# Attention and two expert layers on one core: the last two chunks' rows written in two transfers, and another order of placing expert 0's rows

## The chip, the core and the metric

The kernel runs on one core of a Trainium2 chip. A core has five engines with instruction streams of their own: TensorE (PE, matmuls), VectorE (DVE), ScalarE (ACT), GpSimd (POOL) and SyncE (SP, which here only issues transfers). The streams run in order and wait for each other by semaphores. Transfers between the chip's memory and the on-chip memory run on 16 DMA engines. The metric is the device time of one run in microseconds.

## The reference

Three layers follow each other. Attention with a decaying state (2 batches, 8 heads, 768 tokens, 64 numbers per head), then a mixture of 8 experts in which a token is computed only if a skip score is positive, then a second mixture of 8 experts with a limit of tokens per expert.

```python
for t in range(S):
    state = gamma * state + einsum('bhd,bhe->bhde', k[:, :, t], v[:, :, t])
    y[:, :, t] = scale * einsum('bhd,bhde->bhe', q[:, :, t], state)
# x = y as 1536 rows of 512
do_compute = (x @ w_skip) > 0                      # first mixture
e_idx = argmax(xc @ w_gate)                        # xc: the rows that are computed
h = maximum(xc[mask] @ w1[e], 0.0)                 # 512 x 1024
out[do_compute] = xc + gate_w * (h @ w2[e])        # 1024 x 512
# second mixture: the same shapes, own weights; at most `capacity` rows per expert
```

## The kernel before

Attention runs in 6 chunks of 128 tokens (`NCH = 6`), each with two batches `b`. For every chunk a generator, `sink` in `route_tokens`, follows attention by some steps: it computes the router's logits of the chunk's 256 tokens, picks an expert for each, turns the tokens into rows, and writes the rows with their gates to `table`, an array in the chip's memory. A row of `table` is 516 numbers wide (`RW`): 512 of the token (`DM`), two gates (`GCOL`) and the token's number (`IDCOL`). Later every expert collects its 128 rows from `table` with an indirect transfer (`gather`, issued by GpSimd).

The generator's steps are put between the steps of attention by `step_side`; one step ends at each `yield`. So the order of the instructions on each engine is the order in which the Python code runs.

For chunks 0 to 4, `sink` does this: `logits` (4 matmuls with the router's weights, copied to `lgs` by ACT, L395), a yield, `summed` and `pick` (the choice, on DVE; `ex` on ACT) and `weigh` (the gates: `se` and the reciprocal, L325), a yield, `rows_T` for both batches (4 transposes on TensorE each, L409, and a copy to `rc` by ACT, L413), `write_rows` on ACT's queue (L355), a yield, and then the ranks of the tokens within their experts. In chunk 4, the last of these, it ends with a gather of its own: `a0` gets the rows that expert 0 has from chunks 0 to 4 (L362, with the ids of L477).

The last chunk, 5, has its own code, `last_chunk`. Its rows of expert 0 don't go through `table`: `place` puts them in their slots by a matmul with a one-hot matrix `oh` (L499, `late[0]` for batch 0, `late[1]` for batch 1), and adds `a0` through the identity matrix, all in two accumulators `acc[0]` and `acc[1]` that hold two of the four column blocks each (`KT = 4`, L372). `split` (ACT L378, then DVE L379) turns each accumulator into a high and a low part, `xh` and `xl`, with which the first expert's first layer begins (L794). `warm` is a matmul whose result nobody reads. Chunk 5's rows are written to `table` by SP (L355), ahead of two weight loads (L213) in SP's stream. All later experts' gathers need them.

Rows that are named `rowc_107` and `rowc_108` below are the row buffers of chunk 4 and of chunk 5; `big` are weights as loaded, `hi` and `lo` their parts, `xt` a chunk's attention result, `p` its masked scores, `a_105` the buffer `a0`, and `sbd` the state.

Of the kernel before, what the change touches and what calls it, by code (L numbers as in the profile page):

```python
# [15 lines left out]
B, H, S, D = 2, 8, 768, 64  # L16
NT, DM, E, FF = B * S, H * D, 8, 1024
NCH = S // 128
NTILE = NT // 128
KT = DM // 128  # L20
FT = FF // 128
RW = 516
# [19 lines left out]
def kernel(  # L42
# [12 lines left out]
    nc = tc.nc  # L55
# [9 lines left out]
    at = ExitStack()  # L65
# [3 lines left out]
    table = dram.tile([NROW, RW], F32, name="table")  # L69
# [46 lines left out]
    a0 = const.tile([128, RW], F32, name="a0")  # L116
# [4 lines left out]
    ident = cs[:, C_ID:C_ID + 128]  # L121
# [226 lines left out]

    done = [1]

    def write_rows(eng, src, n):

        r0 = done[0]
        done[0] += 128 * n
        eng.dma_start(out=table[r0:done[0], :].rearrange("(n p) w -> p n w", p=128), in_=src)  # L355

    def gather(at, n=None, t=None):

# [9 lines left out]
    def place(acc, rows, where, first, last, ks=range(KT)):  # L368

        n = KT // len(acc)  # L370
        for k in ks:
            nc.tensor.matmul(  # L372
                out=acc[k // n][:, 128 * (k % n):128 * (k % n) + 128], lhsT=rows[:, 128 * k:128 * k + 128], rhs=where,
                start=first and k % n == 0, stop=last, skip_group_check=True,
            )
# [9 lines left out]
    def route_tokens(rows, rows_p):  # L385
# [26 lines left out]
        def rows_T(xt, rc, b, psum):  # L412
            nc.scalar.activation(out=rc[:, b, 0:DM], in_=turned_rows(xt, b, psum), func=ACTF.Copy)  # L413
# [28 lines left out]
        def sink(c, xt, psum):  # L442
            if c == NCH - 1:
                yield from last_chunk(xt, psum)
                return
            rc = rows[c % len(rows)]
            bs = list(range(B))
            if not c:
                yield
            lgs = logits(xt, bs, psum)  # L450
            nc.gpsimd.tensor_copy(out=rc[:, :, IDCOL:IDCOL + 1], in_=tok[:, :, c:c + 1])
            yield
            lg = summed(lgs, B, psum)
            m, weigh = pick(lg, B, 2, None, rc[:, :, GCOL:GCOL + 2])
            m3 = m.rearrange("p (a g) j -> p a (g j)", a=B)
            weigh()
            rhs = numbers(nc.gpsimd, m3, c, bs)
            yield
            rows_T(xt, rc, 0, psum)
            if c < NCH - 2:  # L460
                yield
            rows_T(xt, rc, 1, psum)
            write_rows(nc.scalar, rc, B)
            yield
            rk = psum("s", 4)
            ranked(rk, lc[:, 0, :], m.rearrange("p n j -> p (n j)"), cum.rearrange("p a j -> p (a j)"))
            sl = slot(rk, m3, B)
            where = [slots_of(sl, i) for i in bs]
            for i in bs:
                counted(m3[:, i, :])  # L470
            yield
            if c < NCH - 2:
                yield
            for i in bs:
                to_slots(where[i], rhs[:, i], 0, 16)
            if c == NCH - 2:
                nc.vector.tensor_copy(out=ids_0[:, 0:1], in_=tab[:, 0:1])  # L477
                gather(ids_0[:, 0:1], t=a0)

        def last_chunk(xt, psum):  # L480

            c = NCH - 1
            rc = rows[c % len(rows)]
            nc.gpsimd.tensor_copy(out=rc[:, :, IDCOL:IDCOL + 1], in_=tok[:, :, c:c + 1])
            m, m2, rhs, late = {}, {}, {}, {}
            ex = ex9[2 * B]

            def picked(b, lgs):
                got, _ = pick(summed(lgs, 1, psum), 1, 2, None, None, ex[:, 2 * b:2 * b + 2])
                m[b] = got.rearrange("p (a g) j -> p a (g j)", a=1)  # L490
                m2[b] = got.rearrange("p n j -> p (n j)")
                rhs[b] = numbers(nc.gpsimd, m[b], c, [b])

            def ranks(b):
                rk = psum("s", 4)
                ranked(rk, lc[:, 0, :], m2[b], cum[:, 0, :], [m2[0]] if b else [])
                sl = slot(rk, m[b], 1)
                oh = rows_p.tile([128, 128], F32, tag="oh", name="oh")
                nc.vector.scalar_tensor_tensor(  # L499
                    out=oh, in0=iota[:, 0:128], scalar=sl[:, 0:1], in1=m[b][:, 0, 0:1].to_broadcast([128, 128]),  # L500
                    op0=ALU.is_equal, op1=ALU.mult,
                )
                late[b] = (rc[:, b, :], oh)
                return sl

            lgs = logits(xt, [0], psum)
            yield
            picked(0, lgs)
            yield
            xr = turned_rows(xt, 0, psum)  # L510
            sl = [ranks(0)]
            lgs = logits(xt, [1], psum)
            nc.scalar.activation(out=rc[:, 0, 0:DM], in_=xr, func=ACTF.Copy)
            warm(psum("s", 4), 1)
            picked(1, lgs)
            rows_T(xt, rc, 1, psum)
            warm(psum("s", 4), 1)
            sl.append(ranks(1))
            acc = [psum("m"), psum("m")]
            place(acc, *late[0], True, False)  # L520
            hi = x_p.tile([128, KT, 128], F32R, tag="xh", name="xh")
            lo = x_p.tile([128, KT, 128], F32R, tag="xl", name="xl")
            gate(ex, B, 2, rc[:, :, GCOL:GCOL + 2])
            write_rows(nc.sync, rc, B)
            for g in range(2):
                ks = slice(2 * g, 2 * g + 2)
                place(acc, *late[1], False, False, range(KT)[ks])
                place(acc, a0, ident, False, True, range(KT)[ks])
                split(acc[g][:, 0:256].rearrange("p (k t) -> p k t", k=2), hi[:, ks], lo[:, ks])
            x0.append((hi, lo))  # L530

            def gather_all():
                where = [slots_of(sl[b], 0, sm, "whereb", 2) for b in range(B)]
                for b in range(B):
                    to_slots(where[b], rhs[b][:, 0], 0, 16)
                nc.vector.tensor_copy(out=ids, in_=tab)
                for e in (1, 0, 2, 3):
                    xs1[e] = gather(ids[:, e:e + 1], 1 + NT)
                for b in range(B):
                    counted(m2[b])  # L540

            x0.append(gather_all)
            yield
# [3 lines left out]
    def warm(acc, n):  # L547

        for _ in range(n):
            nc.tensor.matmul(out=acc, lhsT=zb[:, 0:128], rhs=zb[:, 0:512], start=True, stop=True)  # L550
# [194 lines left out]
    def psum(tag="t", bufs=3):  # L745
        return ps.tile([128, 512], F32, tag=tag, bufs=bufs, name=tag)
# [269 lines left out]
    acc = run(second)  # L1016
    then_route(0, acc)
    for e in range(1, E):
# [12 lines left out]
        if e > 1:  # L1031
# [12 lines left out]
            acc = last_step(second, FT // 2 - (3 if e == E - 1 else 1))  # L1044
# [11 lines left out]
    acc = run(second)  # L1056
# [31 lines left out]
    acc = run(second)  # L1088
# [67 lines left out]
    acc = run(second)  # L1156
# [207 lines left out]
```

## Time and profile before

| | |
|---|---|
| median of 3 runs | 385.44 us (385.2 to 385.46) |
| profiled execution | 384.92 us, of which the span of the profile is 383.1 us |
| TensorE busy | 368.7 us, 96% of the span, granted clock 0.995 on average |
| DVE, ACT, GpSimd busy | 244.7, 213.8, 121.1 us |
| moved by DMA | 95.99 MB, 251 GB/s on average |

An engine's busy time counts its own instructions; waiting and issuing are not busy. The profile's view of the chain that ended last covers only the very end of this program, so stretches, waits and timelines have to tell what bounds the rest. Idle time of an engine that nobody waits for costs nothing. A wait is put down to the last semaphore event that the profile can see; where the engine named had long been done, it was another, often a transfer.

### The profile page before, as it was taken

How to read it: one execution, taken by the hardware profiler on the slowest of the kernel's cores; microseconds unless marked ns; L12 is line 12 of the kernel's file. 1: busy time of each engine (PE TensorE's matmuls, PEld its weight loads, DVE VectorE, ACT ScalarE, POOL GpSimd, SP SyncE). 2: the span in 40 equal slices, each digit the busy share in tenths (PEclk: the TensorE clock that was granted, in tenths of full speed). 3: DMA queues.
4: the chain of work that ended last, by engine and by line, in shares of the span. 5: the costliest groups of instructions: out<-in, count | busy, mean ns of one | idle time of the engine just before them, and what ended most of it. 6: DMA issues, size and time to landing. Idle time of an engine off the chain costs nothing. (4 is left out here: it accounts for less than half of the span.)

```text
span 383.1 us, 6796 instructions
## 1 busy us (share of the span) xinstructions
PE 368.7 (96%) x2641; PEld 311.0 (81%) x2642; DVE 244.7 (64%) x402; ACT 213.8 (56%) x317; POOL 121.1 (32%) x185
## 2 busy tenths in 40 slices
PE   8999999799999999999999999999999999999992
PEld 4788887587777787886678998989899898998981
DVE  3657786479896999899626982747627466473200
ACT  1446554387986777795338763646546454562110
POOL 2677773285042060233251402205031140401102
PEclk9999999999999999999999999999999999999998
DMA  8999976689999999988746784947748386110001
GB/s 292 423 418 399 357 216 230 190 316 379 394 390 397 372 342 350 344 298 323 275 117 188 256 323 150 322 162 216 285 143 307 110 289 242 60 44 28 26 3 43
DMA packets 18128, 95.99 MB, mean 251 GB/s; under 512 B 2401, under 2 KB 2657, under 8 KB 8616
## 3 DMA queue, kind: packets, MB, share of 16 engines
q1 hardware_dynamic: 12196, 80.85, 57.2%
q0 software_dynamic: 3280, 9.76, 8.1%
q10 hardware_dynamic: 2612, 4.86, 3.5%
q8 instruction: 23, 0.38, 0.4%
q14 instruction: 17, 0.14, 0.1%
HBM read 87.03 MB, written 9.48 MB: 252 GB/s over the span
## 5 line engine op out<-in xcount | busy, mean ns | idle before, releaser
L255 DVE TENSOR_TENSOR lo<-big,hi 128x1024 fp32r<-128x1024 f32 (+1 forms) x130 | 151.3, 1185 | 54.1 <-ACT hi L252 53.6
L252 ACT ACTIVATE hi<-big 128x1024 fp32r<-128x1024 f32 (+1 forms) x130 | 128.6, 1015 | 6.9 <-DMA big<-in_w1a_dram 4.0
L788 PE MATMUL s<-xh,lo 128*128 128x256 f32 x224 | 63.4, 283 | 0.0
L787 PE MATMUL s<-xl,hi 128*128 128x256 f32 x224 | 63.4, 283 | 0.0
L786 PE MATMUL s<-xh,hi 128*128 128x256 f32 x224 | 63.4, 283 | 0.0
L924 POOL DMA_INDIRECT out_dram<-y,ixo x16 | 18.6, 1165 | 138.6 <-ACT y L919 136.6
L786 PE MATMUL o<-hi,hTh 128*128 128x512 f32 x112 | 44.2, 394 | 0.0
L788 PE MATMUL o<-hi,hTl 128*128 128x512 f32 x112 | 43.6, 390 | 0.0
L787 PE MATMUL o<-lo,hTh 128*128 128x512 f32 x112 | 43.6, 389 | 0.0
L786 PEld LDWEIGHTS s<-xh,hi 128*128 128x128 f32 x224 | 43.0, 192 | 0.3
L787 PEld LDWEIGHTS s<-xl,hi 128*128 128x128 f32 x224 | 43.0, 192 | 0.3
L788 PEld LDWEIGHTS s<-xh,lo 128*128 128x128 f32 x224 | 43.0, 192 | 0.0
L1124 ACT ACTIVATE hTh<-s 128x512 fp32r<-128x512 f32 x28 | 16.7, 598 | 39.0 <-PE s L788 39.0
L1125 DVE SCALAR_TENSOR_TENSOR hTl<-s,hTh 128x512 fp32r<-128x512 f32 x28 | 19.3, 690 | 28.4 <-ACT hTh L1124 28.4
L919 ACT ACTIVATE y<-o,rowc 128x512 f32<-128x512 f32 (+1 forms) x15 | 10.1, 675 | 45.6 <-issue 29.3
L794 PE MATMUL s<-hi,xh 128*128 128x512 f32 x80 | 32.6, 408 | 0.9 <-DVE xl L379 0.9
L794 PE MATMUL s<-lo,xh 128*128 128x512 f32 x80 | 31.3, 391 | 0.0
L794 PE MATMUL o<-hi,hTh 128*128 128x512 f32 x72 | 29.7, 412 | 0.0
L794 PE MATMUL o<-lo,hTh 128*128 128x512 f32 x72 | 28.2, 391 | 0.0
L794 PE MATMUL s<-hi,xl 128*128 128x512 f32 x80 | 25.0, 394 | 0.0
L788 PEld LDWEIGHTS o<-hi,hTl 128*128 128x128 f32 x112 | 21.0, 188 | 4.4
L787 PEld LDWEIGHTS o<-lo,hTh 128*128 128x128 f32 x112 | 21.1, 188 | 4.2
(162 smaller groups left out, 604.0 us busy)
## 6 DMA issues: line engine op xcount, KB each, us to landing
big<-in_w1a_dram SPq DMA_DIRECT2D x16, 1024.0 KB, 8.8
big<-in_w2a_dram SPq DMA_DIRECT2D x16, 1024.0 KB, 7.1
big<-in_w1b_dram SPq DMA_DIRECT2D x16, 1024.0 KB, 5.4
big<-in_w2b_dram SPq DMA_DIRECT2D x16, 1024.0 KB, 6.0
qk<-in_qkv_dram SPq DMA_DIRECT2D x5, 1024.0 KB, 9.8
big<-in_qkv_dram SPq DMA_DIRECT2D x5, 1024.0 KB, 11.7
table<-rowc ACTq DMA_DIRECT2D x5, 516.0 KB, 6.5
table<-row ACTq DMA_DIRECT2D x3, 516.0 KB, 5.5
```

The lines of the kernel that those rows point to most:

```text
L252: nc.scalar.activation(out=hi[:, k], in_=r3[:, k], func=ACTF.Copy)
L255: nc.vector.tensor_tensor(out=lo[:, k], in0=r3[:, k], in1=hi[:, k].bitcast(F32), op=ALU.subtract)
L786: nc.tensor.matmul(out=acc, lhsT=a[0], rhs=w[0], start=first, stop=False)
L787: nc.tensor.matmul(out=acc, lhsT=a[0], rhs=w[1], start=False, stop=False)
L788: nc.tensor.matmul(out=acc, lhsT=a[1], rhs=w[0], start=False, stop=last)
L794: nc.tensor.matmul(out=acc, lhsT=a, rhs=w, start=first and i == 0, stop=last and i == len(todo) - 1)
L919: nc.scalar.activation(out=y[:, 0:n], in_=acc[:, 0:n], func=ACTF.Copy, scale=xs[:, GCOL + 1:GCOL + 2])
L924: new = nc.gpsimd.indirect_dma_start(out=out[:, :], out_offset=bass.IndirectOffsetOnAxis(ap=ix, axis=0), in_=y, in_offset=None, bounds_che ...
L1124: nc.scalar.activation(out=hi[:, g:g + 2, :], in_=acc, func=ACTF.Relu)
L1125: nc.vector.scalar_tensor_tensor(out=lo[:, g:g + 2, :], in0=acc, scalar=0.0, in1=hi[:, g:g + 2, :].bitcast(F32), op0=ALU.max, op1=ALU.subtract
```

## The change

In chunk 4 the transposes and the copies of the rows come right behind the logits, in the step before the choice is made. The 512 columns of the tokens are issued as one transfer there, and the 4 columns of gates and number as a second transfer once the gates are made; both are on ACT's queue. In chunk 5 the rows are written in the same two parts on SP's queue. And in chunk 5 one `warm` goes, the rows of batch 0 are placed before the ranks of batch 1 are made, and `a0` is placed whole before the rows of batch 1 instead of block by block behind them.

```diff
+    def next_rows(n):
         r0 = done[0]
         done[0] += 128 * n
-        eng.dma_start(out=table[r0:done[0], :].rearrange("(n p) w -> p n w", p=128), in_=src)
+        return table[r0:done[0], :].rearrange("(n p) w -> p n w", p=128)
+
+    def write_rows(eng, src, n):
+        eng.dma_start(out=next_rows(n), in_=src)
...
             lgs = logits(xt, bs, psum)
             nc.gpsimd.tensor_copy(out=rc[:, :, IDCOL:IDCOL + 1], in_=tok[:, :, c:c + 1])
+            if c == NCH - 2:
+                for b in bs:
+                    rows_T(xt, rc, b, psum)
+                at = next_rows(B)
+                nc.scalar.dma_start(out=at[:, :, 0:DM], in_=rc[:, :, 0:DM])
             yield
...
-            rows_T(xt, rc, 0, psum)
             if c < NCH - 2:
+                rows_T(xt, rc, 0, psum)
                 yield
-            rows_T(xt, rc, 1, psum)
-            write_rows(nc.scalar, rc, B)
+                rows_T(xt, rc, 1, psum)
+                write_rows(nc.scalar, rc, B)
+            else:
+                nc.scalar.dma_start(out=at[:, :, DM:RW], in_=rc[:, :, DM:RW])
...
             rows_T(xt, rc, 1, psum)
-            warm(psum("s", 4), 1)
-            sl.append(ranks(1))
+            at = next_rows(B)
+            nc.sync.dma_start(out=at[:, :, 0:DM], in_=rc[:, :, 0:DM])
             acc = [psum("m"), psum("m")]
             place(acc, *late[0], True, False)
+            sl.append(ranks(1))
+            place(acc, a0, ident, False, False)
...
-            write_rows(nc.sync, rc, B)
+            nc.sync.dma_start(out=at[:, :, DM:RW], in_=rc[:, :, DM:RW])
             for g in range(2):
                 ks = slice(2 * g, 2 * g + 2)
-                place(acc, *late[1], False, False, range(KT)[ks])
-                place(acc, a0, ident, False, True, range(KT)[ks])
+                place(acc, *late[1], False, True, range(KT)[ks])
```

ACT, from chunk 4's logits to chunk 5's first copy of `xt`, before:

```order
L395 ACTIVATE lgs<-s 128x256
L309 ACTIVATE ex_118<-d 128x4x8
L413 ACTIVATE rowc_107<-s 128x512 x2
L355 DMA table<-rowc_107 128x2x516
L252 ACTIVATE hi<-big_87 128x512
L681 ACTIVATE xt<-m 128x512
```

The same place after:

```order
L398 ACTIVATE lgs<-s 128x256
L416 ACTIVATE rowc_107<-s 128x512 x2
L460 DMA table<-rowc_107 128x2x512
L309 ACTIVATE ex_118<-d 128x4x8
L474 DMA table<-rowc_107 128x2x4
L252 ACTIVATE hi<-big_87 128x512
L693 ACTIVATE xt<-m 128x512
```

The two copies and the wide transfer moved ahead of `ex`; a second, narrow transfer stands where the one transfer stood.

TensorE at the same place, before (`qk` the second half of chunk 5's first scores, `cs,xt` the transposes, `p,big_88` the outputs of chunk 5):

```order
L391 MATMUL s<-xt,wgt 32x256 x4
L624 MATMUL s<-qk 128x128 x4
L401 MATMUL s<-zsum,lgs 128x18 x2
L665 MATMUL m<-qk,sbd 128x128 x4
L409 MATMUL s<-cs,xt 128x128 x8
L674 MATMUL m<-p,big_88 64x128 x8
```

and after:

```order
L394 MATMUL s<-xt,wgt 32x256 x4
L412 MATMUL s<-cs,xt 128x128 x8
L636 MATMUL s<-qk 128x128 x4
L404 MATMUL s<-zsum,lgs 128x18 x2
L677 MATMUL m<-qk,sbd 128x128 x4
L686 MATMUL m<-p,big_88 64x128 x8
```

The eight transposes moved ahead of the scores, the sums and the state's part.

TensorE at the end of chunk 5, from the transposes of batch 1 to the first expert layer, before (`lc`, `ones` the ranks):

```order
L409 MATMUL s<-cs,xt 128x128 x4
...
L329 MATMUL s<-m,lc 128x16
...
L332 MATMUL s<-m,ones 128x16
L372 MATMUL m<-oh,rowc_108 128x128 x6
L372 MATMUL m<-cs,a_105 128x128 x2
L372 MATMUL m<-oh,rowc_108 128x128 x2
L372 MATMUL m<-cs,a_105 128x128 x2
L794 MATMUL s<-hi,xh 128x512
```

and after:

```order
L412 MATMUL s<-cs,xt 128x128 x4
L375 MATMUL m<-oh,rowc_108 128x128 x4
...
L329 MATMUL s<-m,lc 128x16
...
L332 MATMUL s<-m,ones 128x16
L375 MATMUL m<-cs,a_105 128x128 x4
L375 MATMUL m<-oh,rowc_108 128x128 x4
L806 MATMUL s<-hi,xh 128x512
```

Batch 0's placing moved ahead of the ranks, and all of `a0` ahead of batch 1's rows.

## Rows read from the trace of the kernel before

**Rows 1.** Stretches: start:end, length, busy us per engine, granted clock, DMA share, GB/s.

```profile
core 0: us, PE busy (x) PEld busy (x) DVE busy (x) ACT busy (x) POOL busy (x), PEclk, DMA share, GB/s
66.00:70.00 4.00, 3.00 (x32) 2.15 (x30) 2.37 (x14) 2.07 (x5) 1.70 (x3) 1.00 0.01 5
70.00:74.00 4.00, 2.87 (x22) 2.37 (x20) 1.16 (x6) 0.86 (x3) 0.67 (x5) 1.00 0.83 235
78.00:90.00 12.00, 12.00 (x60) 9.87 (x60) 10.36 (x11) 10.20 (x13) 8.44 (x9) 1.00 0.91 319
90.00:130.00 40.00, 39.23 (x196) 30.73 (x195) 34.94 (x35) 33.87 (x45) 10.24 (x9) 1.00 1.00 392
...
200.00:340.00 140.00, 140.00 (x915) 128.13 (x914) 86.48 (x99) 80.09 (x104) 31.05 (x36) 1.00 0.62 213
```

**Rows 2.** Timeline, 70 to 75 us: start, length, instruction, [idle before <-releaser].

```profile
70.08 0.36 DVE L499 SCALAR_TENSOR_TENSOR oh<-iota,sl,m 128x128 f32<-128x128 f32 x1
...
71.89 0.71 PE L372 MATMUL m<-cs,a 128*128 128x128 f32 x4 [0.62 <-DMA a<-table,ids]
...
72.88 0.61 PE L372 MATMUL m<-cs,a 128*128 128x128 f32 x4
...
74.42 0.50 PE L794 MATMUL s<-hi,xh 128*128 128x512 f32 x1 [0.93 <-DVE xl L379]
```

**Rows 3.** Timeline, 62 to 69 us: chunk 4's write, the ids, the gather.

```profile
62.33 0.37 ACTq L355 DMA_DIRECT2D table<-rowc  x1
...
64.66 0.16 DVE L477 CAST ids<-tab 128x1 int32<-128x1 f32 x1 [0.18 <-PE tab L343]
...
68.25 1.23 POOL L362 DMA_INDIRECT a<-table,ids  x1 [4.59 <-DVE oh L499]
```

**Rows 4.** DMA, four stretches (61.2:63.2, 63.2:64.8, 65.5:66.85, 66.9:70): packets, MB, share; landing.

```profile
q8 instruction: 1, 0.02, 3.1%
...
q10 hardware_dynamic: 231, 0.45, 73.3%
...
q10 hardware_dynamic: 20, 0.04, 7.5%
...
DMA packets 0, 0.00 MB, mean 0 GB/s; under 512 B 0, under 2 KB 0, under 8 KB 0
...
a<-table,ids POOLq DMA_INDIRECT x1, 3.6
```

**Rows 5.** Timeline, 58 to 64 us: chunk 4's rows and gates, chunk 5's first `xt`.

```profile
58.44 0.71 PE L624 MATMUL s<-qk 64*128 64x128 f32 x8
...
60.53 1.04 PE L409 MATMUL s<-cs,xt 128*128 128x128 f32 x8
...
61.17 1.08 ACT L413 ACTIVATE rowc<-s 128x512 f32<-128x512 f32 x2
...
61.84 0.18 DVE L325 RECIPROCAL rowc<-se 128x4 f32<-128x4 f32 x1
...
62.74 0.63 ACT L252 ACTIVATE hi<-big 128x512 fp32r<-128x512 f32 x1 [0.49 <-POOL rhs L429]
...
63.27 0.58 ACT L681 ACTIVATE xt<-m 128x512 f32<-128x512 f32 x1
```

**Rows 6.** DMA, 52.9:57.4 (SP's queue q1), chunk 3's write (7.4), chunk 5's (4.1 us).

```profile
q1 hardware_dynamic: 116, 0.95, 79.3%
...
table<-rowc ACTq DMA_DIRECT2D x1, 516.0 KB, 7.4
...
table<-rowc SPq DMA_DIRECT2D x1, 516.0 KB, 4.1
```

**Rows 7.** Timeline: ACT issues chunk 3's write; SP issues chunk 5's and two loads.

```profile
53.52 0.37 ACTq L355 DMA_DIRECT2D table<-rowc  x1
...
70.91 0.38 SPq L355 DMA_DIRECT2D table<-rowc  x1
...
71.34 1.33 SPq L213 DMA_DIRECT2D big<-in_w1a_dram  x2
```

More of the change, by code (lines that the diff above doesn't have):

```diff
@@ L349 @@
     done = [1]
-    def write_rows(eng, src, n):
+    def next_rows(n):
         r0 = done[0]
         done[0] += 128 * n
-        eng.dma_start(out=table[r0:done[0], :].rearrange("(n p) w -> p n w", p=128), in_=src)
+        return table[r0:done[0], :].rearrange("(n p) w -> p n w", p=128)
+    def write_rows(eng, src, n):
+        eng.dma_start(out=next_rows(n), in_=src)
     def gather(at, n=None, t=None):
```

## The prediction

> **What bounds the kernel now.** I began with TensorE by stretches, since it is busy for nearly the whole span. From 78 us on it has next to no idle time, and the granted clock is 1.00, the 2.4 GHz level. The two stretches from 66 to 74 us stand out, with 3.00 and 2.87 us busy of 4.00 [rows 1]. That is the seam between attention and the first expert layer. Time won or lost there goes to the end one for one, because TensorE has no slack afterwards to take it up.
>
> The timeline of 70 to 75 us says which wait ends last in the seam. TensorE waits 0.62 us for the gathered rows `a0` to land and starts on them at 71.89. It places their second half from 72.88, and the split of that half into `xh` and `xl` on ACT and DVE releases the first expert matmul at 74.42. The rows' other source, the one-hot `oh` of the second half of chunk 5, is ready at 70.44 (70.08 + 0.36), long before [rows 2]. So the gather bounds the seam.
>
> Next, the gather itself. GpSimd starts it at 68.25, after 4.59 us of idle time [rows 3], and its rows land 3.6 us later [rows 4]. The view names `oh` as releaser, but a gather of table rows needs only its list of ids, ready at 64.82 (64.66 + 0.16), and the table rows. The last of those are chunk 4's, issued by ACT at 62.33 [rows 3]. Their 256 pieces of 2,064 B go out over 16 engines, 16 pieces each. The DMA rows by stretches show where they are: 231 packets, nearly all, from 63.2 to 64.8; then 20 stragglers from 65.5 to 66.85 at 7.5% of 16 engines, that is about one engine at work; nothing at all from 66.9 to 70 [rows 4]. That last engine has no weight load left in these 1.35 us and does its 16 pieces in one run, 81 ns each (7.5% x 16 x 1.35 us / 20). I take it that the late one is the engine that also fetched a block of instructions (one packet, 3.1% of 16 engines over 2.0 us, so 0.99 us) between 61.2 and 63.2, in the middle of the weight load issued before; the view doesn't number the engines. The gather follows 1.4 us after its last piece. The wait is thus for the **slowest engine's queue**, not for the moment of issue.
>
> **The change part by part.** *Chunk 4's rows ahead of their gates.* The eight transposes (1.04 us) go from 60.53 to where the second half of the scores started, 58.44 [rows 5]. They end near 59.5. The two copies (1.08 us for both) then end near 60.2 and the 512 columns are issued at about 60.3, 2.0 us earlier than now. What does that win? On 15 engines it wins two microseconds. On the late one nothing, if my reading holds: its earlier queue and the instruction block are untouched, its pieces still come behind the load, and even if they took turns with the load's (8 KB each, 8 per engine by 116 packets for 0.95 MB [rows 6]), 16 pieces outlast 8, so the last one ends when all of that engine's work does, at 66.85. Gain on the gather: 0 in the forecast, at most some 2 us.
>
> *The second transfer of chunk 4.* It holds 256 pieces of 16 B, 16 per engine, and the gather now waits for them too. On the late engine they stand behind the first transfer. Each piece costs between nothing and what a 2,064 B piece costs, 81 ns [rows 4], so 0 to 1.3 us. I take 0.2: the pieces carry under a hundredth of the bytes, but each is still a piece. The Trainium skill, "DMA: Bandwidth & Descriptors", section Specifications, says that a transfer under 512 B is done by reading, modifying and writing back. No write of such pieces to the table is in this trace, so it can neither confirm nor deny it; the page gives no price for it and speaks for the upper end.
>
> *ACT's queue.* The second issue (0.37 us) waits for the gates and stands ahead of one weight split and of chunk 5's `xt` copy. The scores' second half moves by 1.05 us behind the transposes, and with it the mask product, the choice and the gates: reciprocal done at 63.07 instead of 62.02. So the issue runs from 63.1 to 63.5, the split starts near 63.5 instead of 62.74 and `xt` at 64.05 instead of 63.27 [rows 5]. **Everything of chunk 5 comes 0.8 us later**: the last `oh` at 71.25. TensorE waits for that; in the forecast it costs nothing, since `a0` still comes after it. If that cover goes, it bounds the seam (first rival).
>
> *Chunk 5's rows in two transfers.* SP now issues the 512 columns at about 70.1 and the 4 columns near 71.7, and the two weight loads queued behind start at about 72.1 instead of 71.34 [rows 7]. TensorE's next stage moves by as much, so they keep their lead. The gathers that need chunk 5's rows follow ids made after that stage has begun, and the write of now, issued at 70.91, took 4.1 us [rows 6]. Nothing on the path. But the first transfer starts to flow about 70.95, while `a0`'s pieces still do; one or two of its pieces ahead of theirs on an engine are 0 to 0.2 us. I take 0.1.
>
> *The order of placing.* Before, after `a0` lands, two half-places remain besides the one that it starts: (72.88 - 71.89) / 2 = 0.5 us each. Now all of `a0` goes first, and both halves of `oh`'s rows come behind it: three half-places ahead of the last one's start instead of two, with the same 1.54 us from there to the expert layer (72.88 to 74.42) [rows 2]. That is **+0.5 us** as long as `a0` lands last. The one warming matmul that is dropped stood in TensorE's idle time of 66 to 70 us, and so did the ranking matmuls that now follow the first placing: 0. TensorE will be idle for about 2 us before `a0`; the granted clock stayed at 1.00 through 1 us idle per 4 us [rows 1], and I price no fall.
>
> The sum: 0 + 0.2 + 0 + 0.1 + 0.5 = +0.8 us. The profiled execution took 384.92 us (383.1 span and 1.8 around it), so it would become 385.7. It lies 0.5 under the median of the runs, 385.44, which would become 386.2. By bounds: 0 + 0 + 0.5 = +0.5 without any price for the second transfer, 1.3 + 0.2 + 0.5 = +2.0 with the full one.
>
> **The rivals.** *First: the rows land early, and the change does what it is built for.* If the late engine is not late behind an earlier issue, then with the 4.1 us of chunk 5's write [rows 6] the first transfer is there by 64.4 and the second, which holds far fewer bytes, within the same time of 63.1, by 67.2 at the latest. The gather then starts 0.8 to 3 us earlier. It gains from the point where `a0` lands 0.5 us earlier than now, and it gains all where `a0` is placed before the last `oh` comes at 71.25. From there two half-places, the second starting at 71.8, and 1.54 us give 73.35 instead of 74.42: -1.05 us, 384.4. For it: 15 engines of 16 do behave so. Against it: chunk 3's write, issued at 53.52 with a load just ahead, took 7.4 us, and in the 4.5 us to 57.4 only the loads' queue moved packets [rows 6, 7]. The Trainium skill, "DMA: Bandwidth & Descriptors", section Anatomy of one DMA, fits a transfer (one issued by GpSimd) as 2.0 us plus its bytes at 436 GB/s: an estimate from it puts the first transfer down at 63.5 and the second at 65.1, which is this rival's full gain. The 7.4 us of chunk 3 disagree, since the fit knows no queue ahead.
>
> *Second: small pieces are dear.* If the 16 B pieces cost what rows cost, the gather starts 1.3 us later, and the sum is +2.0: 387.4. It is measurable as slower once the second transfer costs more than about 0.2 us.
>
> *Third: the change doesn't tell.* The gather's shift is met by some later wait, as TensorE has 0.77 us idle from 90 to 130 [rows 1]: 385.4.
>
> **How the numbers follow.** The forecast gets 0.54, the first rival 0.21, the second 0.17, the third 0.08. A measurement of this kernel tells about 0.2% from no change, 0.77 us, so 384.67 to 386.21. The forecast sits on the upper edge: its own range is 385.9 to 386.7, a bit under half of it slower. Slower: 0.26 + 0.16 = 0.42. Faster: 0.18 of the first rival, whose gain may be partial. Same: the rest, 0.40. The range reaches from the first rival's full gain to near the second's, 384.4 to 387.2.
>
> **What would show it.** Right: the gather starts at 68.2 to 68.8, stragglers of ACT's queue up to about 67 us, the first expert matmul at about 75.2, `xt` of chunk 5 near 64.05. The first rival: gather before 67.8, TensorE waiting for `oh`, first expert matmul near 73.4. The second: gather near 69.5. I am wrong altogether if chunk 5 is not 0.8 us late, or if the granted clock falls in the seam.

## The result, and the profile of the changed kernel

The changed kernel takes **389.79 us** in the median (389.09 to 393.29, five runs). The kernel before took 385.46 us beside it; the ratio is 1.0109, 95% interval 1.006 to 1.0159. A second comparison gave 389.54 against 386.70 us, 1.0081 (1.0046 to 1.0116). Ratios and intervals leave out a few runs in a slower state and are not quotients of the two medians, from which they differ by up to 0.4%. The forecast was 386.2 us, range 384.4 to 387.2: the side was right, but by the medians the loss is 4.3 and 2.8 us where 0.8 was expected. The profiled execution took 389.09 us, 4.17 us more than that of before (384.92).

Where the 4.2 us sit is read from the stretches (columns as in [rows 1]):

```profile
66.00:70.00 4.00, 3.74 (x47) 2.84 (x46) 2.24 (x14) 1.86 (x5) 1.11 (x1) 1.00 0.06 19
70.00:74.00 4.00, 2.40 (x23) 2.23 (x22) 1.77 (x11) 0.70 (x2) 1.14 (x5) 1.00 0.68 204
...
90.00:130.00 40.00, 37.67 (x185) 29.27 (x184) 33.60 (x34) 31.53 (x42) 10.27 (x9) 1.00 1.00 378
200.00:340.00 140.00, 138.69 (x892) 126.07 (x892) 83.31 (x96) 77.82 (x101) 33.79 (x38) 1.00 0.63 214
```

In [rows 1] TensorE was busy for 39.23 of the 40 us from 90 on, and for all 140 us from 200 to 340. Now it misses 1.56 and 1.31 us more there, far behind the seam that the change edits. The waits of TensorE name both places. After (waited for: us in total, times, longest):

```profile
PE t L887 <- ACT x2t L883: 2.1, 1, 2.1
PE m L375 <- DMA a<-table,ids: 1.6, 1, 1.6
...
PE t L1117 <- DMA rowc<-table,ids_b: 1.3, 1, 1.3
```

and before:

```profile
PE t L875 <- ACT x2t L871: 0.5, 1, 0.5
```

`x2t` holds expert 1's routed rows for the second routing, near 120 us. `rowc` at L1117 holds the rows of the second layer's expert 3, near 250 us; before, nothing waited there.

The rest is in the seam and ahead of it. The timeline of the seam, after (start, length, instruction):

```profile
57.79 0.71 PE L636 MATMUL s<-qk 64*128 64x128 f32 x8
...
64.90 0.58 ACT L693 ACTIVATE xt<-m 128x512 f32<-128x512 f32 x1
...
68.89 1.23 POOL L365 DMA_INDIRECT a<-table,ids  x1 [3.59 <-DVE sl L424]
...
72.78 1.16 PE L375 MATMUL m<-cs,a 128*128 128x128 f32 x8 [1.60 <-DMA a<-table,ids]
...
75.77 0.50 PE L806 MATMUL s<-hi,xh 128*128 128x512 f32 x1 [0.93 <-DVE xl L382]
```

and the row of before that answers to the first of these:

```profile
57.11 0.49 PE L624 MATMUL s<-qk 64*128 64x128 f32 x4
```

At 57 us, ahead of every edit, this execution is already 0.68 us late. The first expert matmul stands at 75.77 against 74.42 [rows 2], +1.35, so the seam itself costs 0.67. The sum: 0.68 + 0.67 + 1.56 + 1.31 = 4.22 us, for 4.2 us in the span (387.3 against 383.1). This is one execution against one execution. Which of the four parts belong to the change is for the experiments to say.

### The profile page after: what moved, and what is told of

Its sections match the earlier page's. It is cut to its first block, busy times and chain, and to the rows that moved or that the text cites. A ratio compares the mean times of both kernels' runs of the same rounds, so it can differ in the third digit from the quotient of the medians.

```text
span 387.3 us, 6799 instructions
## 1 busy us (share of the span) xinstructions
PE 369.6 (95%) x2641; PEld 311.9 (81%) x2641; DVE 244.3 (63%) x402; ACT 213.5 (55%) x317; POOL 119.8 (31%) x185
```

## The experiments

**Three theories** were on record: *Seam* (only the seam is longer, the rest is chance), *Loads*, later *Queue* (the wait for `x2t` grows, since ACT stands behind a late weight load), and *Layout*, later *Collision* (a gather on GpSimd is held up near 244 us). Ratios are to the kernel before, run on the same chip in between; in brackets the 95% interval.

| kernel | median us | before | ratio |
|---|---|---|---|
| again (the change) | 389.54 | 386.70 | 1.0081 [1.0046, 1.0116] |
| c4_only | 386.12 | 386.70 | 0.9990 [0.9963, 1.0017] |
| c5_only | 385.73 | 386.70 | 0.9987 [0.9958, 1.0016] |
| order_only | 386.98 | 386.70 | 0.9991 [0.9949, 1.0033] |
| c4_c5 | 387.67 | 385.51 | 1.0056 [1.0016, 1.0097] |
| c4_order | 387.69 | 385.51 | 1.0040 [1.0004, 1.0075] |
| c5_order | 387.07 | 385.51 | 1.0015 [0.9979, 1.0051] |
| early_two | 385.26 | 385.51 | 0.9996 [0.9954, 1.0039] |
| before_gather_late | 385.98 | 386.09 | 1.0005 [0.9976, 1.0034] |
| after_gather_early | 386.73 | 386.09 | 1.0055 [1.0020, 1.0091] |
| c5_gates_act | 389.31 | 386.09 | 1.0116 [1.0082, 1.0149] |
| before_act_write | 388.97 | 386.09 | 1.0110 [1.0075, 1.0146] |
| before_gather_late6 | 388.49 | 384.73 | 1.0091 [1.0059, 1.0124] |
| before_gather_early | 386.80 | 384.73 | 1.0038 [1.0006, 1.0070] |
| early_c4_gates_sp | 387.33 | 384.73 | 1.0054 [1.0020, 1.0088] |
| x2t_first | 384.14 | 384.73 | 0.9967 [0.9941, 0.9993] |
| after_x2t_first | 384.40 | 385.95 | 0.9962 [0.9937, 0.9987] |
| before_again | 385.22 | 385.95 | 0.9974 [0.9944, 1.0005] |

**How far a ratio can be trusted.** before_again is the kernel before beside itself.

> The kernel before, unaltered, beside itself: 1.000, with an interval of some 0.3% to both sides. If it lies off by as much as before_gather_early did (0.38%), then differences of that size are not to be read as effects in the other runs.

It came out at 0.9974 with half a width of 0.3%. In these comparisons the kernel before alone ran from 382.64 to 389.94 us. A ratio of 0.4% may thus be read as an effect only where a trace shows its place. A profile, in turn, is one execution and need not be a typical one: that of again took 385.26 us, the fastest of its twelve runs (median 389.54), and that of early_two 388.19 us against a median of 385.26. So a profile shows where one execution lost time, not what the median loses.

**The parts, alone and in pairs.** The change has three: chunk 4's early rows in two transfers (c4), chunk 5's write in two (c5), the placing order. Each kernel takes the others back, for instance c4_only from the changed kernel:

```
-            at = next_rows(B)
-            nc.sync.dma_start(out=at[:, :, 0:DM], in_=rc[:, :, 0:DM])
+            warm(psum("s", 4), 1)
+            sl.append(ranks(1))
...
-            nc.sync.dma_start(out=at[:, :, DM:RW], in_=rc[:, :, DM:RW])
+            write_rows(nc.sync, rc, B)
...
-                place(acc, *late[1], False, True, range(KT)[ks])
+                place(acc, *late[1], False, False, range(KT)[ks])
+                place(acc, a0, ident, False, True, range(KT)[ks])
```

In c5_only, order_only and c5_order chunk 4 is as before:

```
-            if c == NCH - 2:
-                for b in bs:
-                    rows_T(xt, rc, b, psum)
...
+            rows_T(xt, rc, 0, psum)
             if c < NCH - 2:
...
+            rows_T(xt, rc, 1, psum)
+            write_rows(nc.scalar, rc, B)
```

> The changed kernel once more, unaltered, to see which of its late places return in a second profile. Theory Loads (the weight loads behind chunk 5's second transfer start late, and their stream has no room from 90 to 130 us): TensorE's wait for x2t near 121 us is again about 2.1 us, against 0.5 us before, whatever else happens. Theory Seam (only the seam between attention and expert 0 is longer, by about 0.8 us, and the rest of the loss is chance): the wait for x2t is back near 0.5 us and the time is near 386.5. In both, the 0.68 us lost at 11 us and the 1.3 us wait for rowc at 252 us may be chance: where they are, they should differ from one profile to the next. Time by Loads 388.5 to 390.5.

> Only chunk 4's part of the change: its rows turned and sent ahead of the gates, in two transfers; chunk 5's write in one and the placing as before. Theory Loads: chunk 5 comes 0.8 us later as in the changed kernel, so the gates and the one write on SP's queue come 0.8 us later and the loads too (issued near 72.1 instead of 71.34); TensorE, which waits for the gather at its old place, doesn't move, so the loads lose 0.8 us of their lead: wait for x2t near 1.3 us, 386.0 to 386.7. Theory Seam: the gather starts as before and the wait for x2t is as before, 385.4 to 385.7.

> Only the write of chunk 5 in two transfers; chunk 4 and the placing as before. Theory Loads: the loads stand behind one more issue (0.4 us) and behind pieces of 16 B, after which the first 8 KB pieces took 1.35 us in the changed kernel, against 0.67 us before; so the loads land about 1 us later and the wait for x2t grows from 0.5 to about 1.5 us: 386.2 to 387. Theory Seam: the gates come when they came before, nothing on the path moves: 385.3 to 385.7.

> Only the placing of expert 0's rows in the other order (a0 ahead of the second half of chunk 5, ranks after the first placing, one warming matmul less); both chunks' writes as before. Theory Seam: the first expert matmul comes 0.5 us later and so does the end: 385.9. Theory Loads: the same in the seam, and the loads keep their place (71.34), so that the wait for x2t shrinks from 0.5 towards 0.1 us and takes most of it back: 385.5.

> Both chunks written in two transfers, the placing as before. Alone, neither of these two parts moved the time (0.999 and 0.9987 of the kernel before), though together with the placing they cost 0.8%. Theory Layout (two more transfers than before change the rhythm of everything behind them: in both profiles of the whole change GpSimd's gather of the second block of expert 2 took 2.04 us instead of 1.01 and TensorE waited 0.9 to 1.3 us for its rows near 250 us, in no profile of a single part): the 2.04 us and the wait return here, about +1.3 us over the kernel before. Theory Loads (chunk 5's second transfer comes 0.8 us later because of chunk 4 and delays the weight loads behind it; a single part keeps within their lead, both don't): TensorE's wait for x2t at 120 us is 2 us or more, and 2 us are lost in the median. Theory Seam (the placing is needed for the loss): within 0.3% of before.

> Chunk 4's rows early in two transfers, and the placing in the new order; chunk 5's write in one. Seam: chunk 5 is 0.8 us late and the new order puts its second half last, so the seam is longer by 0.8 us or more and TensorE idles there longer; most of the loss of the whole change, +2 to +3 us. Layout: one more transfer only, no long gather near 244 us: within 0.3% of before, or the 0.5 us of the order. Loads: no second issue ahead of the loads, within 0.3% of before.

> Chunk 5's write in two transfers and the placing in the new order; chunk 4 as before. Layout: one more transfer only, no long gather near 244 us: within 0.3% of before. Loads: the gates come when they came before, so the loads are 0.4 us later at most: within 0.3%. Seam: the order alone was at 0.9991 of before, with nothing else in the seam later: within 0.3%.

No part alone moved the time. All three cost 0.81%, c4 with c5 0.56%, c4 with the order 0.40%. The three parts alone add up to -0.3%, give or take some 0.6%, against +0.8% for the whole. That speaks against a cost that each part carries for itself, which is how the prediction was summed. As for the wait for `x2t`, it was 0.9 us in the second profile of the change, 2.5 in c4_only, 2.3 in c5_only and 0 in order_only, and Loads' forecast for each part missed. The kernel before had 0.5 us in its first profile and 1.5 in before_again, and 2.0 to 2.4 in four profiles with edits far from this place (early_two and three of the gather kernels below). So this wait jumps from execution to execution, and no run here shows that the change makes it longer. The wait for `rowc` near 250 us is another matter: 1.3 us in the first profile of the change, 0.9 in again, 1.1 in c4_c5, and none at that place in the five that lack c4 or c5. So it goes with these two together.

early_two has as many transfers as the change, the added ones far from the seam:

```
+            if c < 2:
...
+                nc.scalar.dma_start(out=at[:, :, 0:DM], in_=rc[:, :, 0:DM])
+                nc.scalar.dma_start(out=at[:, :, DM:RW], in_=rc[:, :, DM:RW])
+            else:
+                write_rows(nc.scalar, rc, B)
```

> The kernel before, but with the rows of chunks 0 and 1 each written in two transfers, one right behind the other, by ACT, at the place of the old write (near 20 and 30 us). It has as many transfers as the changed kernel and nothing of it in the seam. Layout: the long gather near 244 us (2.04 us) and TensorE's wait near 250 us are there, +1.3 us. Loads and Seam: no difference from before, within 0.2%.

No wait for `rowc`, and 0.9996: the number of transfers isn't it, and Layout falls.

**The held gather.** GpSimd issues the gather of expert 3's second block near 240 us, while DVE starts two pieces of a weight split. Both engines' rows, before:

```profile
241.00 1.01 POOL L362 DMA_INDIRECT rowc<-table,ids_b  x1 [0.30 <-issue]
...
241.21 2.36 DVE L255 TENSOR_TENSOR lo<-big,hi 128x1024 fp32r<-128x1024 f32 x2 [0.25 <-ACT hi L252]
```

and after:

```profile
244.12 2.36 DVE L255 TENSOR_TENSOR lo<-big,hi 128x1024 fp32r<-128x1024 f32 x2 [0.26 <-ACT hi L252]
...
244.19 2.04 POOL L365 DMA_INDIRECT rowc<-table,ids_b  x1 [0.31 <-issue]
```

Before, the gather starts 0.21 us ahead of DVE and takes 1.01 us; after, it starts 0.07 us behind DVE and takes 2.04, and TensorE waits for its rows. Collision says that DVE's piece holds the gather. Two small copies ahead of it, in the kernel before, put that to the test, then six:

```
+                if e == 2 and j:
+                    for _ in range(2):
+                        junk = sm.tile([128, 2], F32, tag="junk", name="junk")
+                        nc.gpsimd.tensor_copy(out=junk, in_=cs[:, 0:2])
                 load_block(e + 1, j)
```

> The kernel before with two small copies (128x2, unused) on GpSimd between the gathers of the two blocks of expert 3 near 240 us, so that the second gather starts about 0.4 us later; nothing else is changed. Theory Collision (a gather that starts inside a 1.2 us piece of DVE's weight split is held until that piece ends; it started 0.16 to 0.21 us ahead of the piece in every kernel without the long gather, 0.07 us behind its start in every kernel with it): the gather takes about 1.8 to 2.0 us instead of 1.01, the end of its rows comes behind the weight load issued near 242.5 us, TensorE waits about 1 us for rowc near 250 us, and the time is 1 to 1.5 us over before. Rival Chance (the long gather has another cause, as the code's place in memory): the gather takes 1.0 us, starts 0.4 us later, and nothing waits: time as before, within 0.2%.

> The kernel before with six small unused copies (128x2) on GpSimd ahead of the second gather near 240 us. Two of them moved its start from 0.21 us ahead of DVE's weight piece to 0.04 us ahead of it, and it still took 1.03 us; six should put it about 0.3 us behind the piece's start. Theory Collision: the gather is held for the 0.9 us that are left of the piece and takes about 1.9 us, its last rows come behind the weight load, and TensorE waits 0.7 to 1.3 us for rowc near 250 us: about +1 us, 1.002 to 1.004 of before. Rival Chance: 1.0 us, no wait, time as before.

With two copies (GpSimd and DVE):

```profile
243.71 1.03 POOL L362 DMA_INDIRECT rowc<-table,ids_b  x1 [0.16 <-issue]
...
243.75 2.36 DVE L255 TENSOR_TENSOR lo<-big,hi 128x1024 fp32r<-128x1024 f32 x2 [0.25 <-ACT hi L252]
```

With six:

```profile
242.83 1.80 POOL L1165 COPY junk<-cs 128x2 f32<-128x2 f32 x6
244.78 1.85 POOL L362 DMA_INDIRECT rowc<-table,ids_b  x1 [0.15 <-PE s L788]
...
243.34 2.39 DVE L255 TENSOR_TENSOR lo<-big,hi 128x1024 fp32r<-128x1024 f32 x2 [0.25 <-ACT hi L252]
```

and TensorE in that one:

```profile
PE t L1105 <- DMA rowc<-table,ids_b: 0.9, 1, 0.9
```

0.04 us ahead of DVE the gather still takes 1.03 us; inside a piece (the second one, which starts near 244.5) it takes 1.85 and TensorE waits, in the kernel before with nothing added but the copies. The ratio goes from 1.0005 to 1.0091. That is more than the 0.9 us of the row, and the six copies took 1.80 us of GpSimd's time, so the gather also started later: this run alone doesn't part the hold from the later start. The other profiles do. In the four in which this gather took 2.04 us (after, again, c4_c5, c5_gates_act) it followed the first gather as closely as in the kernel before, after 1.37 to 1.38 us, and TensorE waited 0.9 to 1.3 us for its rows. In the twelve in which it took 1.01 to 1.03 us with the gathers at their place, TensorE didn't wait for them. That the hold exists and brings the wait is thus shown. The Trainium skill, "SBUF — State Buffer", section "SBUF: two separate sides", gives a reason: VectorE with two SBUF inputs and a GpSimd operation that reads SBUF share one pair of ports, and whichever starts first holds it for the whole instruction. For the gather the rows agree, down to 0.04 us ahead and 0.07 us behind. For DVE they don't: before, it starts 0.21 us into a gather and takes 2.36 us for its two pieces, as long as after.

Then the other way round: the changed kernel with its gathers moved out of DVE's way, and the same move in the kernel before as a control:

```
-        if 1 < e < E - 1:
-            for j in range(2):
-                load_block(e + 1, j)
...
                     emit_out(xs2[e, j], acc[j], e == E - 1 and j > 0)
+                    if e + 2 < E:
+                        load_block(e + 2, j)
```

> The changed kernel, but each block's gather is issued right behind the store that frees its buffer, instead of both behind both stores (L936, then L365, twice), for experts 3 to 7. The gather in question starts near 243 us, while DVE has no weight piece open. Collision: it takes 1.0 us, TensorE doesn't wait for rowc near 252 us, and the time is 1.3 us under the changed kernel's 389.5, about 388.2 (1.005 of before instead of 1.008). Chance: the wait stays or the time doesn't move.

> The kernel before with the gathers issued between the stores as in the kernel after_gather_early: the control for it. Collision: before has no held gather, so there is nothing to win: 1.000 of before, within 0.2%. Rival (the move wins by itself, as the rows land earlier for every expert): 1 us or more faster than before, and then the 1.6 us won on the changed kernel say nothing on the held gather.

Neither profile has the wait for `rowc`, and the changed kernel stands at 1.0055 instead of 1.0081. The control was expected at 1.000 and came out at 1.0038, with no loss behind 130 us in its profile; by before_again such a difference isn't to be leaned on. Against this control the changed kernel is 0.2% slower, which is within the noise. So the size of this part stays loose: 0.9 to 1.3 us by the profiles, and the ratios can't tell it.

**The later place of the seam's transfers.** Three kernels moved a transfer to another queue:

```
c5_gates_act (from the changed kernel)
-            nc.sync.dma_start(out=at[:, :, DM:RW], in_=rc[:, :, DM:RW])
+            nc.scalar.dma_start(out=at[:, :, DM:RW], in_=rc[:, :, DM:RW])
before_act_write (from the kernel before)
-            write_rows(nc.sync, rc, B)
+            write_rows(nc.scalar, rc, B)
early_c4_gates_sp (chunk 4's second transfer; from after_gather_early)
-                nc.scalar.dma_start(out=at[:, :, DM:RW], in_=rc[:, :, DM:RW])
+                nc.sync.dma_start(out=at[:, :, DM:RW], in_=rc[:, :, DM:RW])
```

> The changed kernel, but chunk 5's second transfer (the 4 columns behind the gates) is issued by ACT instead of SP, so that the weight loads don't stand behind it: they are issued near 71.3 instead of 72.8 us. Theory Loads (the weight stream has no room from 90 to 130 us, so that TensorE's wait for x2t near 120 us follows the first load's issue): the x2t matmuls come 1 to 1.5 us earlier against the first expert matmul, and the time is 1 us or more under the changed kernel's, about 388.3. Theory Seam (loads keep their lead, what the seam loses stays lost): 389.5 as the changed kernel.

> The kernel before, but chunk 5's write is issued by ACT instead of SP: the weight loads behind it wait only for their buffers (near 66 us) and not for chunk 5's gates (70.9 us). Loads: 4 to 5 us more lead, no wait for x2t near 120 us (0.5 us in the profile of before, 2.4 us in profiles of slower runs), 0.5 to 1.5 us faster in the median. Rival Contention: the loads' 8 KB pieces flow together with the rows that expert 0 waits for (`a0`, issued near 68 us), which land 1 to 2 us later, and TensorE waits that much longer in the seam: 0.5 us faster to 1.5 us slower.

> The changed kernel with the gathers between the stores, and chunk 4's second transfer issued by SP, whose queue is empty there, instead of ACT. ACT no longer waits for the gates ahead of chunk 5's copy of xt, so chunk 5 comes about 0.4 to 0.8 us earlier in the seam. Theory Seam by ACT: the 1.6 us that after_gather_early has over before shrink by 0.5 to 0.8 us, to about 1.002 of before. Rival Order (the new placing order costs by itself, since both half-places of the last one-hot come behind a0): no change from after_gather_early, 1.005.

None wins anything. c5_gates_act brings the loads to 70.65 us, and its profile has no wait for `x2t`. But the 4 KB behind the gates now come behind two loads of 1 MB (of their queue's packets 168 still move from 78 to 80 us), the gathers of the next experts start at 81.1 instead of 78.1 us, and TensorE waits for them:

```profile
85.90 0.48 PE L777 MATMUL t<-cs,rowc 128*128 128x128 f32 x1 [2.13 <-DMA rowc<-table,ids]
```

before_act_write frees the loads at 64.51 us; they flow together with `a0`, which lands 6.9 us after its issue instead of 3.6 [rows 4], and TensorE waits 2.38 us for it. And although two loads are issued 6 to 7 us earlier there, the wait for `x2t` is 2.6 us: the start of the weight stream doesn't set that wait, and Loads falls in the form in which it was stated. early_c4_gates_sp takes the issue off ACT, and the time is as without it (1.0054 and 1.0055).

**ACT's order near 120 us.** What TensorE waits behind shows in ACT's rows, after:

```profile
121.25 1.06 ACT L252 ACTIVATE hi<-big 128x1024 fp32r<-128x1024 f32 x1 [3.63 <-DMA big<-in_w1a_dram]
122.21 1.06 ACT L883 ACTIVATE x2t<-t 128x512 f32<-128x512 f32 x2
```

and before:

```profile
118.33 1.06 ACT L252 ACTIVATE hi<-big 128x1024 fp32r<-128x1024 f32 x1 [2.94 <-DMA big<-in_w1a_dram]
119.29 1.07 ACT L871 ACTIVATE x2t<-t 128x512 f32<-128x512 f32 x2
```

The copies of `x2t` are ready to run (in the changed kernel TensorE had written what they copy by 116.7 us) but stand behind a split whose weights are still on their way, in both kernels. Two kernels give ACT the copies first; TensorE's own order stays:

```
             next(second)
-            step_side()
             site()
             x = turned(xs1[e + 1] if e + 1 < E else a0, 0, "x")
+            step_side()
```

> The kernel before, but from expert 2 on, where expert 1's routing begins, ACT is given the copies of x2t and of the next expert's xh ahead of the weight split that stands before them now and waits for a weight load (TensorE's own order is the same). Theory Queue (TensorE waits near 120 us because ACT's copies stand behind a split whose load is late; the split weights are not needed yet): the wait for x2t goes, the fall of the granted clock that follows a wait of 2.3 us or more (0.62 to 0.67 for 4 us in three profiles) goes too, and the median is 1.5 to 2.5 us faster than before, 0.994 to 0.996. Rival Stream (the weight stream itself is too slow, and TensorE would wait for split weights a few us later instead): as before, within 0.2%.

> The changed kernel with ACT's copies of x2t and of the next xh ahead of the waiting weight split, as in x2t_first. If the loss behind the seam is partly a longer wait for x2t (theory Queue), this kernel lies no more than the seam's 0.8 us and the held gather's 1.3 us over x2t_first: 1.002 to 1.003 of before. If x2t has no part in it, it lies as far over x2t_first (0.9967) as the changed kernel over before (1.008): 1.005. The held gather (2.04 us) and the wait for rowc near 250 us are there in both cases.

In x2t_first ACT now has:

```profile
115.55 1.09 ACT L871 ACTIVATE x2t<-t 128x512 f32<-128x512 f32 x2
116.50 0.62 ACT L378 ACTIVATE xh<-t 128x512 fp32r<-128x512 f32 x1
119.08 2.01 ACT L252 ACTIVATE hi<-big 128x1024 fp32r<-128x1024 f32 x2 [1.95 <-DMA big<-in_w1a_dram]
...
123.28 2.01 ACT L252 ACTIVATE hi<-big 128x1024 fp32r<-128x1024 f32 x2 [2.19 <-DMA big<-in_w1a_dram]
...
125.45 0.59 ACT L378 ACTIVATE hTh<-t 128x512 fp32r<-128x512 f32 x1
```

The split still waits for its weights, and the wait for `x2t` is gone. But the next pair of splits waits too, until 123.28, the copies `hTh` come only behind them on ACT, and there TensorE waits after all:

```profile
PE o L794 <- DVE hTl L379: 0.8, 1, 0.8
...
PE o L794 <- ACT hTh L378: 0.3, 1, 0.3
```

So Queue is right about the wait for `x2t`, and Stream is right in part: 1.1 us of waiting came back near 127 us. x2t_first stands at 0.9967, a little less than expected; the unaltered kernel came out at 0.9974 beside itself, so this gain isn't clear of the noise. after_x2t_first was expected at 1.002 to 1.005 and came out at **0.9962**, level with x2t_first: with the copies ahead, no loss of the change is left, give or take 0.4%. Its runs also lie closer together (383.63 to 387.30 us, against 385.26 to 393.47 in again). One reservation: its gather near 241 us starts 0.20 us ahead of DVE and takes 1.01 us, so it has no held gather either:

```profile
240.88 1.01 POOL L365 DMA_INDIRECT rowc<-table,ids_b  x1 [0.31 <-issue]
...
241.08 1.23 DVE L255 TENSOR_TENSOR lo<-big,hi 128x1024 fp32r<-128x1024 f32 x1 [0.26 <-ACT hi L252]
```

It therefore shows that the loss isn't tied to the edited rows themselves and goes when ACT's order near 120 us is another. It doesn't show how much of it is the held gather and how much another place.

What becomes of the seam is seen by its side. The first expert matmul and the first transposes near 248 us, x2t_first:

```profile
73.22 0.50 PE L794 MATMUL s<-hi,xh 128*128 128x512 f32 x1 [0.93 <-DVE xl L379]
247.76 1.04 PE L1105 MATMUL t<-cs,rowc 128*128 128x128 f32 x8
```

and after_x2t_first:

```profile
74.75 0.50 PE L806 MATMUL s<-hi,xh 128*128 128x512 f32 x1 [0.93 <-DVE xl L382]
247.94 1.04 PE L1117 MATMUL t<-cs,rowc 128*128 128x128 f32 x8
```

1.53 us apart at the start of the expert layers, 0.18 us apart at 248 us. The place where they meet is the wait of x2t_first near 127 us. In after_x2t_first the same pair of splits gets its weights at nearly the same time, and TensorE, coming later, doesn't wait:

```profile
123.46 2.02 ACT L252 ACTIVATE hi<-big 128x1024 fp32r<-128x1024 f32 x2 [1.07 <-DMA big<-in_w1a_dram]
```

## Why the prediction was wrong

**The step that failed** is the first one: that TensorE "has no slack afterwards", so that time won or lost in the seam "goes to the end one for one". By it the sum had terms for the seam alone, +0.8 us, and none for any place behind it. The runs showed three things in its place.

- *The seam isn't passed on one for one.* In the pair of kernels without the wait for `x2t`, 1.53 us at the start of the expert layers are 0.18 us at 248 us, since the earlier kernel waits 1.1 us near 127 us for weights that are no earlier. The third rival, "the shift is met by some later wait", named this.
- *A place far behind has a cost that the sum has no term for.* The second gather near 240 us starts behind DVE's piece instead of ahead of it and is held, and TensorE waits 0.9 to 1.3 us for its rows.
- *The 0.77 us of idle time that 39.23 in 40 us leaves [rows 1] are no fixed amount.* They held a wait of 0.5 us that hangs on ACT's order and on a full weight stream (DMA share 1.00 from 90 to 130). It was 2.1 us in the change's first profile, 1.56 us of the 4.2, but it jumps as much without the change.

So of the 4.2 us between the two profiles, 1.31 are shown to come with the change, 0.68 stood ahead of every edit, 0.67 lie in the seam, and 1.56 can't be told from chance. What the median loses beyond the held gather, 1.5 to 3.4 us of the 2.8 and 4.3, is not located.

**What bounds the seam.** "So the gather bounds the seam" holds for the profile that was read, and that one was the exception. The same place in before_again:

```profile
57.55 0.72 PE L624 MATMUL s<-qk 64*128 64x128 f32 x8
...
71.47 0.61 PE L372 MATMUL m<-cs,a 128*128 128x128 f32 x4
...
73.90 0.50 PE L794 MATMUL s<-hi,xh 128*128 128x512 f32 x1 [0.93 <-DVE xl L379]
```

It is 0.44 us late at 57 us (57.55 against 57.11). Less that, the first expert matmul stands at 73.46, 0.96 us ahead of [rows 2], and TensorE doesn't wait for `a0`. In six more profiles with chunk 4 and the placing as before (early_two, c5_only, x2t_first and three of the gather kernels) it is the same: 73.45 to 73.48, no wait for `a0`. With the whole change, counted alike, the first expert matmul stands at 75.08 (after), 74.87 (after_x2t_first), 74.55 (after_gather_early), 74.02 (c5_gates_act) and 73.50 (again): 0 to 1.6 us later, by how late the gather's rows come. early_c4_gates_sp, whose profile caught a run of 391.49 us, isn't counted here.

**The gather's start**, forecast unmoved: 68.89 - 0.68 = 68.21 against 68.25. Right in that profile. Counted alike, it started from 66.0 to 68.3 us in the kernels with chunk 4 as before, and from 66.1 to 68.4 in those with its early rows. So the lateness that [rows 4] show is that of some executions only, and the early rows won nothing on the gather in these profiles. In again it started at 66.88 as the first rival has it, but before_again did so without the change (67.03). The reading of one late engine was loose besides: 20 stragglers are more than the 16 pieces of one engine.

**The second transfer**, 0.2 us within 0 to 1.3: its pieces cost next to nothing, and the second rival is wrong. The DMA rows of 66 to 69 us of the changed kernel:

```profile
DMA packets 127, 0.08 MB, mean 25 GB/s; under 512 B 91, under 2 KB 91, under 8 KB 127
...
q10 hardware_dynamic: 126, 0.08, 8.0%
```

126 packets took 8.0% of 16 engines in 3 us, 3.84 us. At 81 ns the 35 large ones make 2.8, which leaves about 11 ns for each small one. The Trainium skill's rule on transfers under 512 B ("DMA: Bandwidth & Descriptors", Specifications) didn't show in their time. The gather does wait for this transfer, though: it landed 4.0 us after its issue at 63.95 and 2.6 us after 63.31 in again, and the gather started 0.9 to 1.0 us behind it in both.

**ACT's queue**, chunk 5 0.8 us late: `xt` at 64.90 against 63.27 [rows 5], less 0.68, so 0.95. Right, and so is its cover in that profile: TensorE waited for `a0`. In c4_only it didn't, and there the first expert matmul stands at 74.40, counted as above, 0.94 us behind the seven.

**The placing order**, +0.5 us, and the seam's +0.8 in all: 0.67 us in the first profile. That the size agrees is luck, since it is measured from the one profile of before in which the gather came late; from the seven others it is 1.6 us there and nothing in again.

**The loads** "keep their lead": they were issued 1.45 us later (72.79 against 71.34 [rows 7]) and TensorE came 1.35 us later, so that was right in this pair. The wait for `x2t` hangs on a load issued near 111 us, in a stream without room.

**The scale**: 385.44 us rested on three runs that happened to lie within 0.3 us. The bound of 0.2% for what can be told was too fine; before_again says some 0.3% for 12 runs.

**Open**: why c4 and c5, harmless alone, together bring the gather 0.28 us later against DVE (it follows a copy of `y` that ACT starts 0.46 instead of 0.18 us behind a split), and where the median of the changed kernel loses what the held gather doesn't explain.

## What to carry to other kernels

A busy share near 1 doesn't say that nothing is slack: look behind the edited place for waits that hang on a full stream or on the order of two engines to a tenth of a microsecond. Before you price a change at a wait, see in a second and third profile of the same kernel that the wait is there; here the wait for the gather stood in one of eight profiles with the same seam. Copies that TensorE waits for belong ahead of work that waits for a load, in the same in-order queue; what that is worth here stayed at the edge of the noise for the kernel before, and the changed kernel was level with it once it had this order. Where parts that are harmless alone cost something together, search the trace for a meeting of two engines.

## What the runs showed of the hardware that was not expected

TensorE's clock: in six of eight profiles in which TensorE waited 2.0 us or more for `x2t`, the granted clock fell right behind the wait. In c4_only (columns as in [rows 1]):

```profile
118.00:122.00 4.00, 2.04 (x9) 1.34 (x8) 1.11 (x2) 1.58 (x3) 0.00 (x0) 1.00 1.02 390
122.00:126.00 4.00, 3.50 (x20) 2.62 (x21) 3.34 (x4) 3.66 (x5) 0.00 (x0) 0.67 0.90 376
```

0.67 is a mix of the two levels, 2.4 and 1.2 GHz; in before_gather_late6 the stretch from 122 to 124 us is at 0.50 throughout. By the starts of the same matmuls ahead of it and behind, it cost 1.4 to 1.6 us in each of the six. In the changed kernel's own profile, with a wait of 2.1 us, and in before_act_write, with 2.6 us, it didn't fall, while it fell behind 2.0 us in before_gather_late6. So the length of the wait alone doesn't decide it, against what was expected for x2t_first, and a wait of about 2 us costs some 2 or 3.5 us from one execution to the next, which is part of the spread of the runs.
